# Two small weights in one tile: 64 runs of nine rows to every second partition, in place of 128 half runs to all of them

## The chip, the core and the metric

The kernel runs on one core of a Trainium2 chip. The metric is the time of one execution on the device in microseconds (us); smaller is better. The core has a matrix engine (TensorE, PE in the profile, with PEld for its weight loads), a vector engine (DVE), an activation engine (ACT), a general engine (POOL) and a queue engine (SP) that issues nearly all transfers. The transfers are carried by 16 DMA engines side by side. On-chip memory has 128 partitions.

## The reference

One decode step: a sum of an input, an attention block with a window of 2048 cached positions, and a mixing and feed-forward block, all on the normalized input. With batch B = 4, width D = 576, 32 query heads over 16 key heads of 128, F = 4608:

```
x  = A_x                                   # (4, 1, 576)
xn = layernorm(x)
# A: q = layernormed x @ wq; scores over the last 2048 of 8192 positions; softmax; p @ v; @ wo
# B: with h = gelu(layernorm(xn) @ w1)       w1: 576 x 576
#    hs = shift(h) @ w2                       w2: 576 x 576; four quarters of h, each shifted along the sequence
#    x1 = xn + hs
#    h2 = gelu(layernorm(x1) @ w3) @ w4       w3: 576 x 4608, w4: 4608 x 576
#    B  = x1 + h2
out = x + A + B
```

The sequence has length one, so every shift of h moves in zeros: the operand of w2 is zero for every input. The kernel still loads w2 and multiplies zeros (`hs_inT`) by it, and computes h.

## The kernel before

Everything is bf16 with fp32 accumulation. The work comes in an order written out by hand: each operation is put in a list of its engine with a sort key, the semaphores that it waits for and the one that it raises; each engine then runs its list in the order of the keys. The SP queue is such a list too, and an entry that waits holds up what is behind it.

The large transfers go to SP in this order: w1, w2, wq, w3, then 16 blocks of keys of 2 MB each (`k_cache`, into four slots of the tile `kring`, where wq lies in slots 2 and 3 at first), then 8 blocks of values of 4 MB each (into `vring` and `kring`), then w4 and five pieces of wo. Key blocks 2 and later wait for the product with wq (signal `q`), blocks 4 and later for the transposes of the block that had the slot, the first two value blocks for the product with w3 (`h2_1`), later ones for the products of the block before them in the slot; w4 and wo wait for value products near the end.

The weights w1, w2, wq and w3 are cut by the function `runs` into 128 runs: nine rows of the weight lie one behind the other in memory, and half of that stretch goes to each partition. For w1 and w2 a run is 4.5 rows, 5184 bytes. A partition then holds the first or the second half of nine rows, so the product's left operand must hold x for two rows at a time, with zeros in the places of the other parity: `pairs` picks the columns of x, `pe_xT` transposes five pieces of it (line 330), `xs_ops` writes two masked copies (line 336) with the parity mask `par`, and `x_at` gives the eight columns for each of the nine steps. `pe_hh` (line 397) computes x @ w1 in 9 matmuls of 288 columns, with the two column halves in rows 0 to 3 and 4 to 7 of the result (`HHps`, one PSUM bank). `pe_hs` (line 405) does the product with w2, two times 9 matmuls. The result of x @ w1 goes through gelu on ACT (line 415, `hh_sb`).

The order on PE at the start: a bank of zeros for q (line 360), the transposes for both layernorms (330), `pe_hh` (397), `pe_hs` for both halves (405) with DVE's sum into `x1_bf` (411) after each, the third layernorm, its transposes (330), the product with wq (369), q's transposes (380), zeros (360), the product with w3 (430), gelu and its transposes (443), zeros for the scores (347). Then come the loops: 16 key blocks (transposes in line 485, scores in line 492), a softmax, 8 value blocks (line 553), and at the end the products with w4 and wo (line 392).

w1 and w2 lie in the tile `ktb`, whose other half POOL sets to zero (line 239) at the start; the key loop uses all of `ktb` later on, and its first write there waits for the two products.

Of the kernel before, what the change touches and what calls it, by code (L numbers as in the profile page):

```python
# [6 lines left out]
BF16 = mybir.dt.bfloat16  # L7
ACTF = mybir.ActivationFunctionType
ALU = mybir.AluOpType
# [28 lines left out]
def bass_parallel_sum__sliding_block_cached__mixer_s_mlp__decode_kernel(  # L38
    nc, A_x, A_k_cache, A_v_cache, A_wq, A_wo, B_x, B_w1, B_w2, B_w3, B_w4, out
):  # L40
    B, Sq, D = A_x.shape
# [16 lines left out]
    HALF = D // 2  # L58
# [11 lines left out]
    with ExitStack() as ctx:  # L70
        def sb(name, shape, dt):
            return ctx.enter_context(nc.sbuf_tensor(name, shape, dt))
# [25 lines left out]
        def cut(n):  # L98
            nonlocal _o
            _o += n  # L100
            return ktb[:, _o - n:_o]
        w1_t = cut(9 * HALF)
        w2_t = cut(9 * HALF)
        assert _o <= NKT // 2 * 1024
        _o = 0
        PTx = vring[:, 4 * UE:4 * UE + 4 * 512].rearrange("p (q x) -> p q x", q=4)
# [9 lines left out]
        sd = sb("sd", [B, 3], FP32)  # L116
        rstd = sb("rstd", [B, 3], FP32)
        xn_bf = sb("xn_bf", [B, D], BF16)
        xp_bf = sb("xp_bf", [B, 3, 5 * 128], BF16)
        x1_bf = sb("x1_bf", [B, D], BF16)  # L120
        xs_t = sb("xs", [128, 3, 22 * B], BF16)
        par = sb("par", [128, 2], FP32)
        hs_inT = sb("hs_inT", [128, 9, 2, B], BF16)
        hh_sb = sb("hh_sb", [2 * B, HALF], BF16)
        h2_sb = sb("h2_sb", [128, 64 * 9], BF16)
        q_sb = vring[:, 5 * UE - 512:5 * UE]
        h2T_sb = sb("h2T_sb", [128, W4R, B], BF16)
# [2 lines left out]
        ident_bf = sb("ident_bf", [128, 128], BF16)  # L130
# [24 lines left out]
        ps = ctx.enter_context(nc.psum_tensor("ps", [128, 8, 512], FP32))[:]  # L155
# [3 lines left out]
        rinvps = ps[:, 5, 0:128]  # L159
        ORps = ps[:, 2, 0:128]  # L160
        ACC = [ps[32 * k:32 * k + B, 7, 0:HALF] for k in range(2)]
        Qps = ps[:, 4, :]
        QTps = ps[:, 0, 0:256].bitcast(BF16).rearrange("p (n j x) -> p n j x", n=4, j=4)
        HSps = ps[0:B, 5, 0:HALF]
        HHps = ps[0:2 * B, 3, 0:HALF]
        TS = ((0, 5), (5, 4))
        H2ps = [ps[:, 4 + k, 0:64 * n] for k, (_, n) in enumerate(TS)]
        H2Tps = ps[:, 1, 0:36 * B].rearrange("p (n j b) -> p n j b", n=9, j=4)
        XTps = [ps[:, k, 0:10].bitcast(BF16).rearrange("p (c b) -> p c b", b=B) for k in range(3)]

        S = {}
        for nm in ("pe", "dve", "act", "pool"):
# [15 lines left out]
        def add(engine, emit, waits=(), sig=None, key=0.0, inc=None):  # L188
            seqc[0] += 1
            prog[engine].append(Op(emit, waits, sig, key, seqc[0], inc))  # L190

        def add_dma(pairs, skey, waits=(), key=0.0, engine="sp"):
            if skey not in S:
                S[skey] = sem("s_" + "_".join(str(k) for k in (skey if isinstance(skey, tuple) else (skey,))))
            dma_count[skey] = dma_count.get(skey, 0) + 16 * len(pairs)

            def emit(e):
                for o_, i_ in pairs:
                    e.dma_start(o_, i_).then_inc(S[skey], 16)  # L199
            add(engine, emit, waits, None, key)  # L200
            return ("dma", skey, dma_count[skey])

        def runs(w_ap):
            return w_ap.rearrange("(m e) n -> m (e n)", e=9).rearrange("m (a x) -> (m a) x", a=2)

        for n in range(NB):
            ev_val[f"T{n}"] = ("T", n + 1)
# [18 lines left out]
        P = lambda *a, **k: add("pool", *a, **k)  # L226

        def pool_ident(t, tag, pattern, view, key):
            P(lambda e: e.memset(t[:], 1.0), sig=tag + "1", key=key)
            P(lambda e: e.affine_select(out=view, in_=view, compare_op=ALU.is_equal, fill=0.0, base=0,  # L230
                                        pattern=pattern, channel_multiplier=1), waits=[tag + "1"], sig=tag, key=key + 0.5)
        P(lambda e: e.memset(zeros_bf[:], 0.0), sig="zeros_bf", key=-100)
        pool_ident(ident_bf, "ident_bf", [[-1, 128]], ident_bf[:], -99)
        P(lambda e: e.memset(Qpad_t[:], 0.0), sig="qpad_zero", key=-96)
        P(lambda e: e.memset(hs_inT[:], 0.0), sig="hs_inT", key=-95.5)
        pool_ident(ident_f, "ident_f", [[-1, 128]], ident_f[:], -95)
# [13 lines left out]
        for gl in range(2):  # L250
            for x in range(2 * NVS):
                v = pick_bf[:, x, gl, 16 * gl:16 * gl + 16].rearrange("p (u r) -> p u r", u=NU)
                P(lambda e, v=v, x=x: e.affine_select(out=v, in_=v, compare_op=ALU.is_equal, fill=0.0, base=-(8 * (x // 2) + x % 2),
                                                      pattern=[[-NI, NU], [-2, 4]], channel_multiplier=1),
                  waits=["pick11"], sig=f"pick2{gl}{x}", key=-84 + 0.1 * (8 * gl + x))


        def mask_of(t, tag, view):
            add("dve", lambda e: e.tensor_reduce(out=t[:], in_=view, axis=AX.X, op=ALU.add), waits=["ident_f"], sig=tag, key=-8)
        add("dve", lambda e: e.tensor_reduce(out=par[:], in_=ident_f[:].rearrange("p (m a) -> p a m", a=2), axis=AX.X, op=ALU.add),  # L260
            waits=["ident_f"], sig="par", key=-29.5)
# [5 lines left out]

        ev_x = add_dma([(x_sb[:], x2)], "x", (), -100, engine="act")
        ev_wq = add_dma([(wq_t, runs(A_wq))], "wq", (), -48)
        ev_w1 = add_dma([(w1_t, runs(B_w1))], "w1", (), -50)  # L270
        ev_w2 = add_dma([(w2_t, runs(B_w2))], "w2", (), -49)
        ev_w3 = add_dma([(w3_t, runs(B_w3))], "w3", (), -47)
        ev_w4 = add_dma([(w4_t, B_w4.rearrange("(p r) n -> p r n", r=W4R))], "w4", [f"PV{2 * (NCV - NVS + 1) + 1}"], KS + NCV)

# [19 lines left out]
        ev_wo, WOR, a = [], [], 0  # L294
# [9 lines left out]
        def ln_ops(idx, src, dst, first_waits, tag, k0):  # L304
            add("dve", lambda e: (e.bn_stats(out=stats[:, idx, 0, :], in_=src[:, 0:HALF]),
                                  e.bn_stats(out=stats[:, idx, 1, :], in_=src[:, HALF:D]))[1],
                waits=first_waits, sig=f"{tag}_st", key=k0)
            add("dve", lambda e: e.bn_aggr(out=mv[:, idx, :], in_=stats[:, idx].rearrange("p a s -> p (a s)")),
                waits=[f"{tag}_st"], sig=f"{tag}_mv", key=k0 + 0.01)
            add("act", lambda e: e.activation(out=sd[:, idx:idx + 1], in_=mv[:, idx, 1:2], func=ACTF.Sqrt, bias=EPS, scale=1.0),  # L310
                waits=[f"{tag}_mv"], sig=f"{tag}_sd", key=k0 + 0.02)
            add("dve", lambda e: e.reciprocal(out=rstd[:, idx:idx + 1], in_=sd[:, idx:idx + 1]),
                waits=[f"{tag}_sd"], sig=f"{tag}_rstd", key=k0 + 0.03)
            add("dve", lambda e: e.tensor_scalar(out=dst[:] if idx == 0 else xp_v(idx), in0=src[:] if idx == 0 else pairs(src),  # L314
                                                 scalar1=mv[:, idx, 0:1], scalar2=rstd[:, idx:idx + 1],
                                                 op0=ALU.subtract, op1=ALU.mult), waits=[f"{tag}_rstd"], sig=f"{tag}_n" if idx == 0 else tag, key=k0 + 0.04)
            if idx == 0:
                add("dve", lambda e: e.tensor_copy(out=xp_v(0), in_=pairs(dst)), waits=[f"{tag}_n"], sig=tag, key=k0 + 0.05)

        xp_v = lambda idx: xp_bf[:, idx, :].rearrange("b (r m a) -> b r m a", r=5, a=2)  # L320

        def pairs(t):
            v = t[:]
            return bass.AP(tensor=v.tensor, offset=v.offset, ap=[list(v.ap[0]), [1, 5], [9, 64], [4, 2]])

        def pe_xT(idx):
            def f(e):
                ins = None
                for r in range(5):
                    ins = e.transpose(XTps[idx][:, r, :], xp_bf[:, idx, 128 * r:128 * (r + 1)], ident_bf[0:B, 0:B])  # L330
                return ins
            return f

        def xs_ops(idx, k0):
            for a in range(2):
                add("dve", lambda e, a=a: e.tensor_scalar(
                        out=xs_t[:, idx, 2 * B * (1 - a):2 * B * (11 - a)].rearrange("p (r v b) -> p r v b", v=4, b=B)[:, :, 0:4:3, :],
                        in0=XTps[idx].unsqueeze(2).to_broadcast([128, 5, 2, B]), scalar1=par[:, a:a + 1], scalar2=None, op0=ALU.mult),
                    waits=([f"xT{idx}"] + ([] if idx else ["par"])) if a == 0 else [], sig=f"xs{idx}{a}", key=k0 + 0.01 * a)

        def x_at(idx, s_):
            return xs_t[:, idx, 2 * B * (s_ + 1):2 * B * (s_ + 2)]

        def pe_zero(e):
            ins = None
# [38 lines left out]
        for k in range(2):  # L384
            for g in range(2):
                add("dve", lambda e, k=k, g=g: e.tensor_copy(
                        out=qp_out[:, :, 2 * k + g].rearrange("p b (j n) y -> p b j n y", j=2),
                        in_=QTps[:, :, 2 * g:2 * g + 2, B * k:B * (k + 1)].rearrange("p (n y) j b -> p b j n y", y=2)),
                    waits=["qTp"] + (["qpad_zero"] if k + g == 0 else []), sig=f"qT{2 * k + g}", key=-10 + 0.1 * k)
# [3 lines left out]

        def pe_hh(e):
            ins = None
            for s_ in range(9):
                ins = e.matmul(HHps, lhsT=x_at(1, s_), rhs=w1_t[:, HALF * s_:HALF * (s_ + 1)], start=(s_ == 0), stop=(s_ == 8))
            return ins
        add("pe", pe_hh, waits=[ev_w1, "xs10", "xs11"], sig="hT", key=-40)

        def pe_hs(h):
            def f(e):
                ins = None
                for s_ in range(9):
                    ins = e.matmul(HSps, lhsT=hs_inT[:, s_, h, :], rhs=w2_t[:, HALF * s_:HALF * (s_ + 1)], start=(s_ == 0), stop=(s_ == 8))
                return ins
            return f
        for h in range(2):
# [3 lines left out]
                waits=[f"hs{h}"], sig="x1" if h else "x1a", key=-27 + 0.1 * h)  # L412
# [3 lines left out]
            waits=["hT", "ln3_sd"], sig="gelu_h", key=-25.9)  # L416
# [30 lines left out]
        for k in range(2):  # L447
            add("pe", pe_h2(k), waits=[ev_w3] + (["xs20", "xs21", "gelu_h", "h2_zero"] if k == 0 else []), sig=f"h2_{k}", key=-18 + k)
            add("act", lambda e, k=k: e.activation(out=h2_v[k], in_=H2ps[k], func=ACTF.Gelu_apprx_tanh), waits=[f"h2_{k}"],
                sig=f"gelu2_{k}", key=-5 + 0.1 * k)  # L450
# [267 lines left out]
```

## Time and profile before

| | us |
|---|---|
| time, median of 3 runs | 213.94 (213.77 to 214.14) |
| the profiled execution's own time | 213.93 |
| its span, first to last instruction | 212.6 |

The profiled execution lies on the median; 1.3 us of its time are outside the span. In the profile's lines "PE L397" is a matrix product of line 397; SPq and ACTq are the queues that issue transfers; "x9" is a count. In a timeline the first two numbers are the start and the duration in us, and the brackets at the end tell how long the engine was idle before and what ended it. In the table of windows each engine has its busy time with its count of instructions, then come the granted clock, the mean busy share of the 16 DMA engines, and GB/s. A packet's bytes are counted where it is recorded, so that in short windows the share can be over 1.

### The profile page before, as it was taken

How to read it: one execution, taken by the hardware profiler on the slowest of the kernel's cores; microseconds unless marked ns; L12 is line 12 of the kernel's file. 1: busy time of each engine (PE TensorE's matmuls, PEld its weight loads, DVE VectorE, ACT ScalarE, POOL GpSimd, SP SyncE). 2: the span in 40 equal slices, each digit the busy share in tenths (PEclk: the TensorE clock that was granted, in tenths of full speed). 3: DMA queues.
4: the chain of work that ended last, by engine and by line, in shares of the span. 5: the costliest groups of instructions: out<-in, count | busy, mean ns of one | idle time of the engine just before them, and what ended most of it. 6: DMA issues, size and time to landing. Idle time of an engine off the chain costs nothing.

```text
span 212.6 us, 4856 instructions
## 1 busy us (share of the span) xinstructions
PE 172.5 (81%) x2212; PEld 133.7 (63%) x2216; DVE 111.9 (53%) x168; ACT 58.6 (28%) x69; POOL 15.6 (7%) x38
## 2 busy tenths in 40 slices
PE   1456147999999999999996089999989598997495
PEld 0222014888878888887774048988868487883262
DVE  5433200477776777777764869995575444003000
ACT  2004001366665566666656520000000000000000
POOL 8991000000000000000000000000000000000000
PEclk9997855899999999999999589999999889999799
DMA  6999999999999999999999999999999999999993
GB/s 242 453 444 445 429 396 416 432 425 427 429 416 438 432 422 429 435 422 424 432 444 438 444 407 459 413 425 453 407 444 438 419 425 410 451 476 393 407 408 131
DMA packets 5066, 88.65 MB, mean 417 GB/s; under 512 B 568, under 2 KB 704, under 8 KB 1216
## 3 DMA queue, kind: packets, MB, share of 16 engines
q1 hardware_dynamic: 5040, 88.49, 97.7%
q8 instruction: 8, 0.13, 0.3%
q14 instruction: 2, 0.02, 0.0%
q10 hardware_dynamic: 16, 0.01, 0.0%
HBM read 88.49 MB, written 0.00 MB: 416 GB/s over the span
## 4 chain that ended last, share of the span: by engine, by line
DMA 47%; PE 45%; DVE 4%; SPq 1%; ACT 1%; issue 1%
PE ps L485 23%; DMA vring<-in_A_wo_dram 15%; DMA vring<-in_B_w_dram 13%; DMA vring<-in_A_v_cache_dram 12%; PE ps L553 11%; DMA kring<-in_A_k_cache_dram 7%; PE ps L492 6%; PE ps L430 2%; SPq L199 1%; DVE vring L520 1%; DVE rmax L498 1%; DVE ktb L545 1%; PE ps L514 1%; PE ps L347 1%; ACT ktb L468 0%
## 5 line engine op out<-in xcount | busy, mean ns | idle before, releaser
L469 DVE COPY ktb<-ps 128x1024 bf16<-128x1024 bf16 x80 | 53.8, 689 | 23.5 <-PE ps L485 23.4
L485 PEld LDWEIGHTS ps<-perm_bf,kring 128*128 128x128 bf16 x1024 | 58.2, 98 | 8.3 <-issue 7.6
L485 PE MATMUL ps<-perm_bf,kring 128*128 128x128 bf16 x1024 | 61.7, 220 | 0.2
L468 ACT ACTIVATE ktb<-ps 128x1024 bf16<-128x1024 bf16 x48 | 48.0, 1023 | 32.5 <-PE ps L485 32.1
L545 DVE TENSOR_TENSOR ktb<-kring,mH_bf 128x4096 bf16<-128x4096 bf16 x16 | 36.2, 2286 | 14.6 <-PE ps L553 14.6
L553 PE MATMUL ps<-vring,ktb 128*128 128x256 bf16 x256 | 30.3, 282 | 4.3 <-DMA vring<-in_A_v_cache_dram 3.5
L553 PEld LDWEIGHTS ps<-vring,ktb 128*128 128x128 bf16 x256 | 25.7, 101 | 8.5 <-issue 3.6
L553 PE MATMUL ps<-kring,ktb 128*128 128x256 bf16 x256 | 28.6, 273 | 0.9 <-DMA kring<-in_A_v_cache_dram 0.9
L553 PEld LDWEIGHTS ps<-kring,ktb 128*128 128x128 bf16 x256 | 25.0, 98 | 4.5 <-issue 1.1
L608 ACT ACTIVATE out_sb<-ps 4x288 bf16<-4x288 f32 x1 | 0.4, 399 | 84.6 <-PE ps L392 84.6
L492 PE MATMUL ps<-ktb,Qs 128*32 128x512 bf16 x272 | 17.8, 382 | 1.2 <-ACT ktb L468 1.2
L430 PE MATMUL ps<-vring,xs 128*8 128x320 bf16 (+1 forms) x72 | 4.5, 429 | 7.6 <-DMA vring<-in_B_w_dram 7.6
L492 PEld LDWEIGHTS ps<-ktb,Qs 128*32 128x32 bf16 x272 | 5.7, 96 | 6.7 <-DVE ktb L469 1.4
L514 PE MATMUL ps<-vring,pick_bf 128*32 128x256 bf16 x64 | 3.9, 411 | 6.4 <-DVE rinv L532 6.4
L609 DVE CAST out_sb<-ps 4x288 bf16<-4x288 f32 x1 | 0.4, 449 | 15.7 <-PE ps L392 15.7
L392 PE MATMUL ps<-vring,h2T_sb 128*4 128x288 bf16 x72 | 6.2, 347 | 3.1 <-DMA vring<-in_B_w_dram 3.1
L571 DVE TENSOR_SCALAR tmp<-ps,maskd 128x128 f32<-128x128 f32 x2 | 0.7, 350 | 14.8 <-PE ps L553 14.8
L430 PEld LDWEIGHTS ps<-vring,xs 128*8 128x8 bf16 x72 | 2.1, 110 | 9.8 <-DMA vring<-in_B_w_dram 8.0
L330 PE MATMUL ps<-ident_bf,xp_bf 4*128 4x4 bf16 x15 | 0.8, 163 | 8.1 <-DVE xp_bf L314 5.0
L392 PEld LDWEIGHTS ps<-vring,h2T_sb 128*4 128x4 bf16 x72 | 3.7, 101 | 5.8 <-DMA vring<-in_B_w_dram 3.6
L514 PEld LDWEIGHTS ps<-vring,pick_bf 128*32 128x32 bf16 x64 | 2.0, 118 | 8.2 <-DVE rinv L532 6.9
L239 POOL MEMSET ktb<- 128x8192 bf16 x1 | 6.9, 6924 | 0.0
(93 smaller groups left out, 78.6 us busy)
## 6 DMA issues: line engine op xcount, KB each, us to landing
kring<-in_A_k_cache_dram SPq DMA_DIRECT2D x16, 2048.0 KB, 13.8
vring<-in_A_v_cache_dram SPq DMA_DIRECT2D x4, 4096.0 KB, 24.6
kring<-in_A_v_cache_dram SPq DMA_DIRECT2D x3, 4096.0 KB, 34.0
vring<-in_B_w_dram SPq DMA_DIRECT2D x2, 5184.0 KB, 25.1
kring<-in_A_wq_dram SPq DMA_DIRECT2D x1, 4608.0 KB, 15.7
kring<-in_A_v_cache_dram SPq DMA_DIRECT2D x2, 2048.0 KB, 27.4
vring<-in_A_wo_dram SPq DMA_DIRECT2D x1, 1872.0 KB, 26.9
vring<-in_A_wo_dram SPq DMA_DIRECT2D x1, 1440.0 KB, 29.8
```

Of the source, the lines that this page charges most:

```text
L199: e.dma_start(o_, i_).then_inc(S[skey], 16)
L239: P(lambda e: e.memset(ktb[:, NKT // 2 * 1024:NKT * 1024], 0.0), key=-92, inc=(("E", LB - 2), 1))
L347: ins = e.matmul(ps[:, w, :], lhsT=zeros_bf[:, 0:128], rhs=zeros_bf[:, :], start=True, stop=True)
L392: return e.matmul(ACC[h], lhsT=lhsT, rhs=rhs, start=start, stop=stop, tile_position=(0, 32 * h), skip_group_check=True)
L430: ins = e.matmul(H2ps[k][32 * j:32 * j + 2 * B].rearrange("b (p t) -> b p t", t=n), lhsT=x_at(2, s_), rhs=w[:, :, 9 * j + t0:9 * j + t0 + ...
L468: return "act", lambda e: e.activation(out=ktbuf[:, n % NKT], in_=tb[n % 4], func=ACTF.Copy)
L469: return "dve", lambda e: e.tensor_copy(out=ktbuf[:, n % NKT], in_=tb[n % 4])
L485: ins = e.transpose(tb[j % 4][:, t, :], kslot_t(k)[:, 8 * kb + t, :], perm_bf[:])
L492: ins = e.matmul(Sps[32 * u:32 * u + 32, q, :].rearrange("p (t i) -> p t i", t=16), lhsT=Qs[:, k, 32 * u:32 * u + 32], rhs=ktgrp[:, (4 * k ...
L514: ins = e.matmul(ps[32 * j:32 * j + 32, 4 + qt, 256 * ih:256 * (ih + 1)].rearrange("p (t a e) -> p t a e", a=NPAIR, e=2), lhsT=pick_bf[:, ...
L545: return lambda e: e.tensor_tensor(out=PTpad[:, n % 4], in0=PTv[:, qt, NH * h:NH * (h + 1), bp, :].unsqueeze(2).to_broadcast([128, NH, NX, ...
L553: ins = e.matmul(ps[:, 0, 0:256], lhsT=PTpad[:, 2 * (k % 2) + h, 2 * g:2 * g + 2].rearrange("p t h e -> p (t h e)"), rhs=vslot(k)[:, Dh * ...
```

## The change

w1 and w2 are no longer cut in half runs. Each goes in 64 runs of nine whole rows, 10368 bytes, w1 to the even partitions and w2 to the odd partitions of one tile, `w12_t`. The tile has the same number of bytes per partition as the two tiles before.

A product over all 128 partitions therefore meets both weights. For w1 the left operand holds x on the even partitions and zeros on the odd ones: POOL sets a new tile `xw_bf` to zero first, the second layernorm writes to every second place of it (`nines` picks the columns), nine transposes in place of five bring it to `xw_t`, and one DVE copy takes the place of the two masked ones. `pe_hh` needs 18 matmuls, nine for each half of the columns, into two PSUM banks, and waits for w2 as well as for w1. For w2 the operand is zero everywhere, as before. The gelu covers 4 partitions with 576 columns in place of 8 with 288. The result of q moves to another PSUM bank.

```diff
-        w1_t = cut(9 * HALF)
-        w2_t = cut(9 * HALF)
+        w12_t = cut(9 * D)
...
-        xp_bf = sb("xp_bf", [B, 3, 5 * 128], BF16)
+        xp_bf = sb("xp_bf", [B, 2, 5 * 128], BF16)
+        xw_bf = sb("xw_bf", [B, 9, 64, 2], BF16)
+        xw_t = sb("xw", [128, 9, B], BF16)
...
-        hs_inT = sb("hs_inT", [128, 9, 2, B], BF16)
-        hh_sb = sb("hh_sb", [2 * B, HALF], BF16)
+        hs_inT = sb("hs_inT", [128, 9, B], BF16)
+        hh_sb = sb("hh_sb", [B, 2, HALF], BF16)
...
-        Qps = ps[:, 4, :]
+        Qps = ps[:, 6, :]
...
-        HHps = ps[0:2 * B, 3, 0:HALF]
+        HHps = ps[0:B, 3:5, 0:HALF]
...
+        def rows9(w_ap):
+            return w_ap.rearrange("(m e) n -> m (e n)", e=9)
+
         def runs(w_ap):
-            return w_ap.rearrange("(m e) n -> m (e n)", e=9).rearrange("m (a x) -> (m a) x", a=2)
+            return rows9(w_ap).rearrange("m (a x) -> (m a) x", a=2)
...
+        P(lambda e: e.memset(xw_bf[:], 0.0), sig="xw_zero", key=-97)
         P(lambda e: e.memset(Qpad_t[:], 0.0), sig="qpad_zero", key=-96)
...
-        ev_w1 = add_dma([(w1_t, runs(B_w1))], "w1", (), -50)
-        ev_w2 = add_dma([(w2_t, runs(B_w2))], "w2", (), -49)
+        ev_w1 = add_dma([(w12_t[0:128:2], rows9(B_w1))], "w1", (), -50)
+        ev_w2 = add_dma([(w12_t[1:128:2], rows9(B_w2))], "w2", (), -49)
...
+        def nines(t):
+            v = t[:]
+            return bass.AP(tensor=v.tensor, offset=v.offset, ap=[list(v.ap[0]), [1, 9], [9, 64]])
+
         def pe_xT(idx):
+            src = xw_bf[:].rearrange("b e m a -> b (e m a)") if idx == 1 else xp_bf[:, idx // 2, :]
...
-                for r in range(5):
-                    ins = e.transpose(XTps[idx][:, r, :], xp_bf[:, idx, 128 * r:128 * (r + 1)], ident_bf[0:B, 0:B])
+                for r in range(9 if idx == 1 else 5):
+                    ins = e.transpose(XTps[idx][:, r, :], src[:, 128 * r:128 * (r + 1)], ident_bf[0:B, 0:B])
...
         def xs_ops(idx, k0):
+            if idx == 1:
+                add("dve", lambda e: e.tensor_copy(out=xw_t[:], in_=XTps[1]), waits=["xT1"], sig="xw", key=k0)
+                return
...
-            for s_ in range(9):
-                ins = e.matmul(HHps, lhsT=x_at(1, s_), rhs=w1_t[:, HALF * s_:HALF * (s_ + 1)], start=(s_ == 0), stop=(s_ == 8))
+            for h in range(2):
+                for s_ in range(9):
+                    ins = e.matmul(HHps[:, h, :], lhsT=xw_t[:, s_, :], rhs=w12_t[:, D * s_ + HALF * h:D * s_ + HALF * (h + 1)],
+                                   start=(s_ == 0), stop=(s_ == 8))
             return ins
-        add("pe", pe_hh, waits=[ev_w1, "xs10", "xs11"], sig="hT", key=-40)
+        add("pe", pe_hh, waits=[ev_w1, ev_w2, "xw"], sig="hT", key=-40)
...
-                    ins = e.matmul(HSps, lhsT=hs_inT[:, s_, h, :], rhs=w2_t[:, HALF * s_:HALF * (s_ + 1)], start=(s_ == 0), stop=(s_ == 8))
+                    ins = e.matmul(HSps, lhsT=hs_inT[:, s_, :], rhs=w12_t[:, D * s_ + HALF * h:D * s_ + HALF * (h + 1)], start=(s_ == 0), stop=(s_ == 8))
```

More of the change, by code (lines that the diff above doesn't have):

```diff
@@ L118, in bass_parallel_sum__sliding_block_cached__mixer_s_mlp__decode_kernel @@
         xn_bf = sb("xn_bf", [B, D], BF16)
-        xp_bf = sb("xp_bf", [B, 3, 5 * 128], BF16)
+        xp_bf = sb("xp_bf", [B, 2, 5 * 128], BF16)
+        xw_bf = sb("xw_bf", [B, 9, 64, 2], BF16)
+        xw_t = sb("xw", [128, 9, B], BF16)
         x1_bf = sb("x1_bf", [B, D], BF16)
-        xs_t = sb("xs", [128, 3, 22 * B], BF16)
+        xs_t = sb("xs", [128, 2, 22 * B], BF16)
         par = sb("par", [128, 2], FP32)
-        hs_inT = sb("hs_inT", [128, 9, 2, B], BF16)
-        hh_sb = sb("hh_sb", [2 * B, HALF], BF16)
+        hs_inT = sb("hs_inT", [128, 9, B], BF16)
+        hh_sb = sb("hh_sb", [B, 2, HALF], BF16)
         h2_sb = sb("h2_sb", [128, 64 * 9], BF16)
@@ L168, in bass_parallel_sum__sliding_block_cached__mixer_s_mlp__decode_kernel @@
         H2Tps = ps[:, 1, 0:36 * B].rearrange("p (n j b) -> p n j b", n=9, j=4)
-        XTps = [ps[:, k, 0:10].bitcast(BF16).rearrange("p (c b) -> p c b", b=B) for k in range(3)]
+        XTps = [ps[:, k, 0:2 * n].bitcast(BF16).rearrange("p (c b) -> p c b", b=B) for k, n in enumerate((5, 9, 5))]
         S = {}
@@ L313, in ln_ops @@
                 waits=[f"{tag}_sd"], sig=f"{tag}_rstd", key=k0 + 0.03)
-            add("dve", lambda e: e.tensor_scalar(out=dst[:] if idx == 0 else xp_v(idx), in0=src[:] if idx == 0 else pairs(src),
+            add("dve", lambda e: e.tensor_scalar(out=dst[:] if idx == 0 else xw_bf[:, :, :, 0] if idx == 1 else xp_v(idx),
+                                                 in0=src[:] if idx == 0 else nines(src) if idx == 1 else pairs(src),
                                                  scalar1=mv[:, idx, 0:1], scalar2=rstd[:, idx:idx + 1],
-                                                 op0=ALU.subtract, op1=ALU.mult), waits=[f"{tag}_rstd"], sig=f"{tag}_n" if idx == 0 else tag, key=k0 + 0.04)
+                                                 op0=ALU.subtract, op1=ALU.mult), waits=[f"{tag}_rstd"] + (["xw_zero"] if idx == 1 else []), sig=f"{tag}_n" if idx == 0 else tag, key=k0 + 0.04)
             if idx == 0:
                 add("dve", lambda e: e.tensor_copy(out=xp_v(0), in_=pairs(dst)), waits=[f"{tag}_n"], sig=tag, key=k0 + 0.05)
-        xp_v = lambda idx: xp_bf[:, idx, :].rearrange("b (r m a) -> b r m a", r=5, a=2)
+        xp_v = lambda idx: xp_bf[:, idx // 2, :].rearrange("b (r m a) -> b r m a", r=5, a=2)
         def pairs(t):
@@ L334, in xs_ops @@
         def xs_ops(idx, k0):
+            if idx == 1:
+                add("dve", lambda e: e.tensor_copy(out=xw_t[:], in_=XTps[1]), waits=["xT1"], sig="xw", key=k0)
+                return
             for a in range(2):
                 add("dve", lambda e, a=a: e.tensor_scalar(
-                        out=xs_t[:, idx, 2 * B * (1 - a):2 * B * (11 - a)].rearrange("p (r v b) -> p r v b", v=4, b=B)[:, :, 0:4:3, :],
+                        out=xs_t[:, idx // 2, 2 * B * (1 - a):2 * B * (11 - a)].rearrange("p (r v b) -> p r v b", v=4, b=B)[:, :, 0:4:3, :],
                         in0=XTps[idx].unsqueeze(2).to_broadcast([128, 5, 2, B]), scalar1=par[:, a:a + 1], scalar2=None, op0=ALU.mult),
@@ L341, in x_at @@
         def x_at(idx, s_):
-            return xs_t[:, idx, 2 * B * (s_ + 1):2 * B * (s_ + 2)]
+            return xs_t[:, idx // 2, 2 * B * (s_ + 1):2 * B * (s_ + 2)]
         def pe_zero(e):
```

## The prediction, made before the result was known

> **What bounds the kernel now.** I read first the page's second and third parts: what the 16 DMA engines did over the span, and what each queue moved.
>
> ```profile
> span 212.6 us, 4856 instructions
> ...
> DMA  6999999999999999999999999999999999999993
> ...
> DMA packets 5066, 88.65 MB, mean 417 GB/s; under 512 B 568, under 2 KB 704, under 8 KB 1216
> ...
> q1 hardware_dynamic: 5040, 88.49, 97.7%
> ```
>
> The DMA row holds a 9 in every slice but the first and the last: the 16 engines never run dry. The queue of SP, q1, moves 88.49 MB and fills 97.7% of the engines' time. So the kernel takes as long as its bytes take, plus some 2 us before the first of them and 3 after the last. To see whether that holds in each stage I take the windows, where the last three columns are the granted clock, the share of the DMA engines and GB/s:
>
> ```profile
> core 0: us, PE busy (x) PEld busy (x) DVE busy (x) ACT busy (x) POOL busy (x), PEclk, DMA share, GB/s
> 1.50:2.50 1.00, 0.48 (x1) 0.00 (x0) 0.26 (x1) 1.00 (x1) 0.97 (x2) 1.00 0.64 150
> 2.50:5.00 2.50, 0.00 (x0) 0.00 (x0) 2.13 (x7) 0.39 (x2) 2.35 (x7) 1.00 1.03 406
> 6.20:20.00 13.80, 8.29 (x73) 4.04 (x73) 5.88 (x17) 1.88 (x3) 10.32 (x23) 0.94 1.01 434
> 20.00:94.00 74.00, 64.45 (x1062) 51.38 (x1056) 41.90 (x80) 35.88 (x38) 0.00 (x0) 0.90 1.00 425
> 178.00:208.00 30.00, 25.81 (x254) 18.79 (x255) 2.53 (x6) 0.00 (x0) 0.00 (x0) 0.94 1.00 425
> ```
>
> From 2.5 us on every stage has a share of 1.00 or more, at 406 to 434 GB/s, while the matrix engine's load changes from nothing to nearly everything. Third, the chain of waits in order of time (start, length, what):
>
> ```profile
> 2.17 27.46 DMA vring<-in_B_w_dram
> 29.63 0.04 issue
> 29.68 4.52 PE ps L430 x56
> ...
> 92.14 2.35 PE ps L485 x40
> 94.49 0.02 issue
> 94.51 14.58 DMA kring<-in_A_k_cache_dram
> ...
> 142.08 25.49 DMA vring<-in_A_v_cache_dram
> ...
> 178.35 31.68 DMA vring<-in_A_wo_dram
> ```
>
> It begins with w3, which stands in the queue behind w1, w2 and wq and lands at 29.63. In between there are stretches of PE work, but each DMA link is far longer than the transfer itself: the 2048 KB block issued at 94.51 needs about 5 us at 425 GB/s and lands after 14.58, because others stand before it. A link like that is a full queue. So whatever the change adds to or takes from the time in which w1 and w2 go through the engines moves w3, the keys, the values and the end by the same amount; what it does elsewhere counts only if it makes an issue so late that the queue empties.
>
> **The transfers of w1 and w2.** What they take now:
>
> ```profile
> L199 SPq DMA_DIRECT2D ktb<-in_B_w_dram x2: 374/395/416, 0.8 to 1.2; - x2
> ...
> DMA to landing us min/median/max: 3.6/4.3/5.0
> ```
>
> w1 is issued at 0.80 and lands 3.6 us later at 4.4, w2 is issued at 1.24 and lands 5.0 later, at 6.2. Together they are 2 x 648 KB = 1.327 MB. The bytes stay the same; 256 packets of 5184 bytes become 128 of 10368, and each transfer now goes to 64 partitions in place of 128.
>
> Half as many packets: the window with nothing but w1 and w2 in it (2.5 to 5.0) runs at 406 GB/s, the ones with large rows at 425 to 434. If the longer runs closed the whole gap to 434, 1.327 MB would take 3.06 us in place of 3.27: a gain of 0.2. I take 0.1, the middle between that and nothing.
>
> Half as many partitions: this is the term that decides, and no row shows it. Every large transfer of this kernel writes all 128 partitions. The fastest long window, 434 GB/s, is 3.4 GB/s for one partition. To keep its time the change needs 6.8 GB/s for each partition that it writes, twice what any row shows. Bounds: at one end nothing is lost, because the engines are the limit and not the place that they write to; at the other end a partition takes no more than it is seen to take. At that end, w1 and w2 go at half of 406, 203 GB/s. In the window from 1.5 to 2.5 only 0.15 MB arrive, at 150 GB/s, less than that half, so those bytes lose nothing. The other 1.177 MB take 5.80 us in place of 2.90: a loss of 2.9 us (3.3 if nothing hides at the start). I take a value near this end, because it is what the rows nearest to it bear out: 16 engines together have been seen to write to 128 partitions only. I don't take all of it. [...] Loss: 2.9 - 0.4 = 2.5 us, with 0 and 3.3 as ends.
>
> [...]
>
> **The work on the engines.** All of it lies between the landing of w2 and the landing of w3. The rows that carry the path and its cover:
>
> ```profile
> 7.39 0.29 PE L330 MATMUL ps<-ident_bf,xp_bf 4*128 4x4 bf16 x5 [1.98 <-DVE xp_bf L314]
> 8.46 2.32 PE L397 MATMUL ps<-ktb,xs 128*8 128x288 bf16 x9 [0.78 <-DVE xs L336]
> 17.32 0.40 ACT L415 ACTIVATE hh_sb<-ps 8x288 bf16<-8x288 f32 x1
> 17.41 3.06 PE L369 MATMUL ps<-kring,xs 128*8 128x512 bf16 x36
> 21.57 0.54 PE L360 MATMUL ps<-zeros_bf 128*128 128x320 bf16 x2
> 29.68 4.49 PE L430 MATMUL ps<-vring,xs 128*8 128x320 bf16 x72 [7.56 <-DMA vring<-in_B_w_dram]
> 36.26 1.49 PE L347 MATMUL ps<-zeros_bf 128*128 128x512 bf16 x3 [0.81 <-DVE h2T_sb L452]
> ```
>
> - Wait added: `pe_hh` also waits for w2. Now w2 lands at 6.2 and the product starts at 8.46, held by x. In the slow case w2 lands at about 8.7 to 9.5, so up to 1.0 us later; queued behind it on PE are the product with w2, the third layernorm's transposes and the product with wq.
> - Matmuls: 18 of 288 columns in place of 9. The 9 take 2.32 us at the start; at that price the others add 2.3.
> - Transposes: 9 in place of 5, at 0.29 for 5: +0.24. The gelu has 576 columns in place of 288, at most twice 0.40: +0.4, beside the transposes and the product with wq.
>
> Sum on PE's path: 1.0 + 2.3 + 0.2 + 0.4 = 3.9 us at most. PE sits idle for 7.56 us before the product with w3, waiting for w3's landing and for nothing else. So it costs nothing, with 3.6 us to spare, and more in the slow case, where w3 lands later as well. Were the cover gone, each us would be paid in full.
>
> What is issued later: the third key block waits in SP's queue for the end of the product with wq, and all later issues stand behind it.
>
> ```profile
> SPq L199 <- PE ps L369: 16.5, 1, 16.5
> ...
> 1.78 1.83 POOL L234 MEMSET Qpad<- 128x2080 bf16 x1
> 3.91 0.40 POOL L230 TENSOR_SCALAR_AFFINE_SELECT ident_f<-ident_f 128x128 f32<-128x128 f32 x1
> 5.54 6.92 POOL L239 MEMSET ktb<- 128x8192 bf16 x1
> 13.84 2.80 POOL L253 TENSOR_SCALAR_AFFINE_SELECT pick_bf<-pick_bf 128x16 bf16<-128x16 bf16 x16
> ...
> 6.41 0.93 DVE L314 TENSOR_SCALAR xp_bf<-xn_bf,mv,rstd 4x640 bf16<-4x640 bf16 x1
> 7.64 0.68 DVE L336 TENSOR_SCALAR xs<-ps,par 128x40 bf16<-128x40 bf16 x4
> ```
>
> That wait ends at 17.41 + 3.06 = 20.5, by the sum above at 24.4 at the latest. In the queue then stand what is left of w3, until 29.63, and two key blocks, 2 x 5 us: the engines have work until about 39. 15 us of cover; nothing lost.
>
> POOL's new fill of `xw_bf` has 1152 elements per partition; at Qpad's 1.83 us for 2080 that is 1.0 us. It stands ahead of Qpad, so all of POOL's later work comes 1.0 later. The second layernorm's write (6.41) needs the fill by then and has it at about 2.8. The parity mask, on DVE just before the copies at 7.64, needs `ident_f`, ready at 4.31, then 5.3. The zeros in `ktb` end at 13.5 in place of 12.46 and are needed by the key loop, which starts after 36.26 + 1.49. The last selection ends at 17.6 and is needed after the keys. Nothing lost. On DVE one copy of 36 columns replaces two masked ones of 40: at most 0.3 us gained, into the same cover. The moved PSUM bank has no price, and the space per partition is the same.
>
> **The sum**, against the profiled execution's own 213.93, which lies on the median of 213.94: +2.5 for the partitions, -0.1 for the packets, 0 for the rest: 216.3 us.
>
> **The rivals.** *The engines are the limit, not the partitions.* For it: the rate hardly depends on what is transferred, 425 in the key stage and 425 at the end, and 64 rows can still be dealt to 16 engines, four each. Against: no row has a partition taking 6.8 GB/s. Then only the packets count: 213.93 - 0.1 = 213.8, no change. [...] That the transfer is cut in other pieces than the diff says, and so isn't changed at all, ends here too. Chance 0.29.
>
> *Faster: long runs pay more than I give them.* w2 lands 1.8 us after w1 (6.2 against 4.4), where its bytes need 1.53 us at 434 GB/s. If that 0.27 us goes for both transfers, the end comes 0.5 us earlier: 213.4. Against: each landing is that of the last of 16 engines, so the gap holds their spread too, which longer runs need not narrow. Chance 0.11.
>
> *Slower by PE.* If the path of 3.9 us grew beyond 7.56, the product with w3 and the key loop, in which PE works without a gap until 94.5, would come later. But the queue is full there, so only what then empties it counts: 1 us beyond the cover gives at most 214.9. It needs a wait that I don't see. Chance 0.04.
>
> **How the numbers follow.** My forecast, half the partitions at about half the rate, has 0.56; its own range goes from half of the loss, 1.4, to the whole of 3.3: 215.3 to 217.2. With the first rival it holds 0.85; the range that takes in both goes from 213.5 to 217.2. Below it lies the faster case. About 0.2%, 0.43 us, is what a measurement of this kernel can tell from no change; the three runs before differ by 0.37. Faster: 0.11. Same: 0.29. Slower: 0.56 + 0.04 = 0.60.
>
> **What would show it.** Right: w2 lands near 8.7 in place of 6.2, the windows from 2.5 to 8 show about 200 to 250 GB/s, w3 lands near 32, and the DMA links of the chain keep their lengths while each starts 2.5 us later. PE's idle time before the product with w3 stays between 5 and 8 us. The prediction is wrong if w3 lands within 0.3 us of 29.6, if the added time appears in the key or value stage instead, or if PE doesn't wait for w3.

## The result, and the profile after

The changed kernel takes 215.00 us in the median of 8 runs (214.47 to 215.71) against 213.97 for the kernel before: a ratio of 1.0053, 95% interval 1.0038 to 1.0067. It is slower by 1.0 us, clear of noise, where 2.4 was forecast. Its runs also spread more: 1.2 us from the fastest to the slowest, where before's have 0.4. The profiled execution took 215.69, near the slow end of them, with a span of 214.4; a second profile of the same kernel, further down, took 215.03.

The page's parts on the span and the transfers:

```profile
span 214.4 us, 4882 instructions
...
DMA  6999989999999999999999999999999999999991
...
DMA packets 4938, 88.65 MB, mean 413 GB/s; under 512 B 568, under 2 KB 704, under 8 KB 960
...
q1 hardware_dynamic: 4912, 88.49, 97.0%
```

The same 88.49 MB in 128 packets fewer, and an 8 now stands in the sixth slice of the row. The windows, with the columns of before:

```profile
1.50:2.50 1.00, 0.49 (x1) 0.00 (x0) 0.04 (x1) 1.00 (x1) 0.96 (x2) 1.00 0.54 119
2.50:5.00 2.50, 0.00 (x0) 0.00 (x0) 2.12 (x6) 0.39 (x2) 2.44 (x4) 1.00 0.91 365
2.50:8.00 5.50, 0.27 (x5) 0.21 (x5) 4.79 (x11) 0.59 (x3) 5.29 (x10) 1.00 1.09 415
6.20:20.00 13.80, 7.64 (x50) 4.28 (x50) 5.64 (x16) 1.69 (x4) 11.34 (x24) 1.00 0.94 400
20.00:94.00 74.00, 65.30 (x1081) 50.72 (x1080) 42.25 (x82) 36.20 (x39) 0.00 (x0) 0.93 1.00 427
178.00:208.00 30.00, 25.41 (x241) 18.86 (x245) 1.93 (x6) 0.00 (x0) 0.00 (x0) 0.94 1.00 428
```

From 20 us on the rate is that of before (427 for 425, 428 for 425): the loss is made ahead of that. But w1 and w2 don't go at half rate: 365 GB/s in place of 406 in their window, and 119 in place of 150 in the one before. The window from 6.2 to 20, which is mostly wq's, has 400 in place of 434: one engine lands w2 1.9 us after the middle one of the 16 and one lands wq 1.4 us after the middle one (in the kernel before 0.4 for both), and wq's first packets take longer too (up to 2380 ns, in the kernel before up to 1974). The transfers themselves, with the key issues of before in the first row, and the chain:

```profile
L199 SPq DMA_DIRECT2D kring<-in_A_k_cache_dram x16: 534/535/616, 2.7 to 94.5; - x16
...
L200 SPq DMA_DIRECT2D kring<-in_A_k_cache_dram x16: 534/535/1640, 3.1 to 95.2; - x16
...
L200 SPq DMA_DIRECT2D ktb<-in_B_w_dram x2: 553/562/571, 0.8 to 1.4; - x2
...
DMA to landing us min/median/max: 4.0/5.3/6.7
```

```profile
2.66 28.80 DMA vring<-in_B_w_dram
31.45 0.04 issue
31.50 4.25 PE ps L447 x52
...
75.87 14.45 DMA kring<-in_A_k_cache_dram
...
142.93 25.70 DMA vring<-in_A_v_cache_dram
...
178.22 34.02 DMA vring<-in_A_wo_dram
```

An issue of 64 runs occupies SP for 0.55 to 0.57 us where one of 128 took 0.37 to 0.42. w1 lands at 0.8 + 4.0 = 4.8 in place of 4.4, w2 at 1.4 + 6.7 = 8.1 in place of 6.2, w3 at 31.45 in place of 29.63. One of the key issues took 1640 ns where none took more than 616 before: SP was held up. The later links of the keys and the values keep about their lengths (14.45 for 14.58, 25.70 for 25.49). The last one doesn't, 34.02 for 31.68: it is another piece of wo, and by the semaphore records one engine lands that piece at 212.25 where the other 15 have it by 211.44. So part of what this execution takes over the median comes from its very end.

The work on the engines came out as the prediction priced it:

```profile
1.78 1.05 POOL L238 MEMSET xw_bf<- 4x1152 bf16 x1
...
8.37 0.40 PE L342 MATMUL ps<-ident_bf,xw_bf 4*128 4x4 bf16 x9 [2.35 <-DVE xw_bf L319]
9.22 4.48 PE L413 MATMUL ps<-ktb,xw 128*4 128x288 bf16 x18 [0.46 <-DVE xw L348]
...
20.00 0.64 ACT L432 ACTIVATE hh_sb<-ps 4x576 bf16<-4x576 f32 x1
...
PE ps L447 <- DMA vring<-in_B_w_dram: 6.8, 1, 6.8
```

The fill takes 1.05 us (1.0 was estimated), the 18 matmuls 4.48 (2.3 + 2.3), the gelu 0.64. PE still waits 6.8 us for w3.

The views show only the last of 16 engines to land a transfer. Read out of the trace's packet and semaphore records, for the two small weights (a transfer "lands" on each engine by itself; a packet's record doesn't name its engine):

```
kernel               packet  median ns  slowest   second transfer lands, first to last engine
before               5184 B     199        831      5.70 to 6.22
changed             10368 B     389       1304      6.05 to 8.14
e4, changed again   10368 B     396       1435      5.93 to 7.47
e1 transfers alone  10368 B     392       1219      6.00 to 7.45
e3 two halves       10368 B     780        824      8.79 to 9.15
e7 behind wq        10368 B     389        389     16.68 to 17.29
```

In the changed kernel most packets take 389 ns, hardly less than two of before's 199. But while the second transfer runs one packet takes 1304 ns (1435 in e4), and one engine lands that transfer 1.9 us (1.4 in e4) after the middle one of the 16. In e1 it is two engines. By the semaphore records each of the large transfers behind them has 16 landings of its own as well, so an engine that is late can stay so to the end: in e4's profile, an execution of 215.03 us, the 16 engines land the last piece of wo 0.4 us later than before's in the mean, and the last of them 1.2 us later.

### The profile page after: what moved, and what is told of

Read it like the earlier page. It is cut to its first block, busy times and chain, and to the rows that moved or that the text cites. A ratio compares the mean times of both kernels' runs of the same rounds, so it can differ in the third digit from the quotient of the medians.

```text
span 214.4 us, 4882 instructions
## 1 busy us (share of the span) xinstructions
PE 172.0 (80%) x2225; PEld 133.2 (62%) x2229; DVE 112.6 (53%) x167; ACT 59.3 (28%) x69; POOL 16.7 (8%) x39
## 3 DMA queue, kind: packets, MB, share of 16 engines
q1 hardware_dynamic: 4912, 88.49, 97.0%
HBM read 88.49 MB, written 0.00 MB: 413 GB/s over the span
## 4 chain that ended last, share of the span: by engine, by line
DMA 55%; PE 36%; DVE 4%; SPq 2%; ACT 1%; issue 1%
PE ps L502 17%; DMA vring<-in_A_wo_dram 16%; DMA kring<-in_A_k_cache_dram 14%; DMA vring<-in_B_w_dram 13%; DMA vring<-in_A_v_cache_dram 12%; PE ps L570 10%; PE ps L509 5%; PE ps L447 2%; SPq L200 2%; DVE vring L537 1%; DVE rmax L515 1%; DVE ktb L562 1%; PE ps L531 1%; ACT ktb L485 0%; PE ps L362 0%
## 5 line engine op out<-in xcount | busy, mean ns | idle before, releaser
L502 PEld LDWEIGHTS ps<-perm_bf,kring 128*128 128x128 bf16 x1024 | 57.4, 98 | 8.7 <-issue 7.1
L570 PE MATMUL ps<-vring,ktb 128*128 128x256 bf16 x256 | 28.6, 273 | 4.5 <-DMA vring<-in_A_v_cache_dram 3.7
L570 PEld LDWEIGHTS ps<-vring,ktb 128*128 128x128 bf16 x256 | 24.8, 98 | 7.9 <-issue 3.6
```

Source lines behind the costliest of these rows:

```text
L502: ins = e.transpose(tb[j % 4][:, t, :], kslot_t(k)[:, 8 * kb + t, :], perm_bf[:])
L570: ins = e.matmul(ps[:, 0, 0:256], lhsT=PTpad[:, 2 * (k % 2) + h, 2 * g:2 * g + 2].rearrange("p t h e -> p (t h e)"), rhs=vslot(k)[:, Dh * ...
```

## The experiments

Each was timed against the kernel before on the same chip; its medians there were 213.71 to 213.97. The theory at first: the loss lies in the transfers, in the start and not in the partitions' rate. The rivals: the partitions' rate (the prediction's term), and the added work on the engines.

**Transfers alone, work alone (e1, e2).** e1 is the kernel before with this:

```diff
-        ev_w1 = add_dma([(w1_t, runs(B_w1))], "w1", (), -50)
-        ev_w2 = add_dma([(w2_t, runs(B_w2))], "w2", (), -49)
+        ev_w1 = add_dma([(w12_t[0:128:2], rows9(B_w1))], "w1", (), -50)
+        ev_w2 = add_dma([(w12_t[1:128:2], rows9(B_w2))], "w2", (), -49)
```

(`w1_t` and `w2_t` are now the two halves of that tile's columns, and `pe_hh` also waits for w2.)

> The kernel before with the changed transfers alone: w1 and w2 go as 64 runs of nine rows to alternate partitions; the products stay the old 9 steps of 288 columns over that tile, so x @ w1 is not what the reference has. If the whole loss lies in the transfers (my theory), this is as slow as the changed kernel: 1.0 us over before (214.8 to 215.5), w2 lands near 8 us and w3 near 31 us. If it lies in the longer work on PE and POOL (rival), it stays at before's 214.0, with w3 at 29.6.

Measured: 214.97 us, ratio 1.0047 (1.0030 to 1.0065), with w2 landing at 7.45 and w3 at 30.64. e2 is the changed kernel with the opposite edit (`w12_t[:, 0:9 * HALF]` and `runs(B_w1)`, and so for w2):

> The changed kernel with the transfers of before: 128 half runs of w1 and w2 to all partitions; the 18 matmuls, nine transposes and the fill of the changed kernel stay, over a layout that they do not fit, so x @ w1 is not what the reference has. If the transfers are the whole loss: 214.0, as before, with w3 at 29.6. If the added work costs, up to 215.0.

Measured: 213.98 us, ratio 1.0002 (0.9993 to 1.0010). The whole loss is in the transfers; the added work costs nothing. One sign was missed, the landing of w3:

```profile
2.17 28.84 DMA vring<-in_B_w_dram
31.01 0.04 issue
```

It comes at 31.01, almost as late as in the changed kernel, and the end is that of the kernel before. By the semaphore records 15 of the 16 engines have w3 by 29.56, and one is 1.4 us later. A fetch of 16 KB of instructions, 0.94 us long, is on record at 23.0; the kernel before has its first such fetch at 33.6, and there one engine lands the first key block 1.2 us after the others (35.70). That such a fetch holds up one engine fits, but isn't shown. So a late landing of w3 is no proof of a loss: it is the landing of one engine of 16, and at the end another may be the last.

**The changed kernel again (e4)**, without an edit:

> The changed kernel unchanged, for a second profile: its eight times lie between 214.47 and 215.71. If one late engine in w2 (landing 8.1 in the first profile) belongs to the layout, w2 lands near 8 again; if that was chance, it lands near 6.6, 0.35 after before's, and the profiled time is near 214.5.

Measured: 215.15 us (214.28 to 216.24), ratio 1.0061 (1.0042 to 1.0080); w2 landed at 7.5, and a key issue took 1111 ns. The late engine is no chance of one profile.

**Halves in place of alternate partitions (e3)**, to see whether it matters where the 64 partitions lie:

```diff
-        ev_w1 = add_dma([(w12_t[0:128:2], rows9(B_w1))], "w1", (), -50)
-        ev_w2 = add_dma([(w12_t[1:128:2], rows9(B_w2))], "w2", (), -49)
+        ev_w1 = add_dma([(w12_t[0:64], rows9(B_w1))], "w1", (), -50)
+        ev_w2 = add_dma([(w12_t[64:128], rows9(B_w2))], "w2", (), -49)
...
-        xw_bf = sb("xw_bf", [B, 9, 64, 2], BF16)
+        xw_bf = sb("xw_bf", [B, 9, 2, 64], BF16)
```

> The changed kernel with w1 on partitions 0 to 63 and w2 on 64 to 127 in place of even and odd ones; all products as in the changed kernel. [...] If the loss is only a late start and one late engine, whatever the partitions are: 215.0, as the changed kernel.

Measured: 216.72 us, ratio 1.0125 (1.0111 to 1.0140): 2.8 us slower than before. The window of w1 and w2, that of the kernel before first, and e3's landings:

```profile
2.50:8.00 5.50, 0.56 (x10) 0.42 (x10) 4.67 (x15) 0.59 (x3) 5.29 (x9) 1.00 1.08 429
...
2.50:8.00 5.50, 0.27 (x5) 0.21 (x5) 4.79 (x11) 0.59 (x3) 5.29 (x10) 1.00 1.06 245
...
DMA to landing us min/median/max: 5.2/6.5/7.7
```

This is the half rate of the prediction, at nearly the size that it gave (2.5): 245 GB/s in place of 429, each packet 780 ns in place of 389, w2 at 9.1. (16 packets of 10368 bytes in 780 ns are 213 GB/s; the end of the window has the first of wq in it.) But it belongs to neighbours. Alternate partitions don't have it.

**Half runs on the alternate partitions (e5)**, to see whether the long packets matter: the tile gets 64 more columns, and each partition's row is cut in two.

```diff
-        w12_t = cut(9 * D)
+        w12_t = cut(9 * D + 64)
...
-        ev_w1 = add_dma([(w12_t[0:128:2], rows9(B_w1))], "w1", (), -50)
+        ev_w1 = add_dma([(w12_t[0:128:2].rearrange("m (a x) -> m a x", a=2)[:, :, 0:9 * HALF],
+                          rows9(B_w1).rearrange("m (a x) -> m a x", a=2))], "w1", (), -50)
```

(and so for w2, with the products' columns moved along)

> The changed kernel with the same 64 alternate partitions, but each partition's nine rows come in two runs of 5184 bytes with a gap of 64 bytes between them, so there are 128 packets per transfer again. If the long packets make one engine late, it is gone and the time is near before's plus the later start, 214.3. If the 64 partitions do (fewer rows per engine, other places), 215.0, with w2's landing at 7.4 or later.

Measured: 215.01 us, ratio 1.0056 (1.0044 to 1.0069), w2 landing at 7.4. The loss doesn't come from the length of the packets.

**The other one first (e6)**: the keys of w1 and w2 in the queue exchanged.

> The changed kernel with w2 issued ahead of w1. If the late engine belongs to what is second in the queue, 215.0 again, with the second transfer's landing at 7.4 to 8.1 and the first's at 4.8. If it belongs to w2's rows or the odd partitions, the first transfer lands late, near 6, and the second near 7.

Measured: 214.80 us, ratio 1.0053 (1.0036 to 1.0069). The second transfer, now w1, lands at 1.4 + 6.5 = 7.9. The first lands at 5.1, somewhat late. What is second is hit, whichever weight it is and on even or odd partitions.

**Another place in the queue (e7, e8, e10, e12).** e7: the changed kernel with `"wq", (), -48` turned into `-51`, so that wq goes first. e8: the same in the kernel before.

> The changed kernel with wq issued first, then w1, w2, w3. If the loss is a late start of the first transfer (an issue of 0.55 us in place of 0.37) it vanishes, since wq's issue is not longer: 214.0 or e8's time. If the late engine comes with these transfers wherever they stand, 0.5 to 1.0 over e8. PE gets to the product with w3 later, by about 3 us after w3's landing; the queue stays full, so I expect no cost of that.

> The kernel before with wq issued first, the control for e7: 214.0 if the order of the first four transfers does not matter, as the full queue says.

Measured: e7 213.97 us, ratio 1.0003 (0.9994 to 1.0011); e8 214.04, ratio 1.0008 (0.9999 to 1.0017). The loss is gone. A window inside w1 and w2, that of e8 first, and e7's landings, then PE:

```profile
13.90:15.40 1.50, 0.00 (x0) 0.00 (x0) 0.00 (x0) 0.00 (x0) 1.50 (x9) 1.00 1.03 429
...
13.90:15.40 1.50, 0.00 (x0) 0.00 (x0) 0.00 (x0) 0.00 (x0) 1.37 (x7) 1.00 1.03 435
...
DMA to landing us min/median/max: 14.5/15.0/15.5
...
32.93 3.55 PE L447 MATMUL ps<-vring,xs 128*8 128x320 bf16 x72
```

435 GB/s to 64 alternate partitions is 6.8 GB/s for each, the rate that no row of before had; the same window of e8, with 128 partitions, has 429. (Towards its end some engines are at w2 already, on the other 64 partitions. The middle engine lands w2 1.56 us after w1, which is four packets of 389 ns, and the first packet of w1 starts at 13.25: up to 14.8 no engine should be at w2, and from 13.80 to 14.80 the rate is 435 too.) The last row shows something more: the product with w3 starts at 32.93, 3.3 us later than in the kernel before, and w3 has been there since 29.6. PE is 3.3 us late at the key loop, and that costs nothing.

e12 puts the halves of e3 behind wq:

> The version on partitions 0 to 63 and 64 to 127, with wq issued first. If neighbours share ways into the memory wherever the transfer stands in the queue, the loss is that of the first such run, about 2.8: 216.8. If that loss too came from the start, 214.0.

Measured: 217.45 us, ratio 1.0166 (1.0151 to 1.0181). That is 3.5 us over before, more than the 2.8 that I expected; the packets take 780 ns here too. The neighbours' loss is there in either place in the queue.

e10 leaves w1 first and moves only w2 behind wq (key -47.5 in place of -49):

> The changed kernel with the order w1, wq, w2, w3. If each of the two transfers at the start costs by itself (late start by w1, one late engine in w2), only the late start is left: 214.2 to 214.3. If one transfer of 64 runs at the start is enough for the whole loss, 215.0.

Measured: 213.98 us, ratio 1.0004 (0.9995 to 1.0012). I had expected the late start to stay, and it doesn't:

```profile
L200 SPq DMA_DIRECT2D kring<-in_A_k_cache_dram x16: 534/535/620, 3.3 to 95.8; - x16
L200 SPq DMA_DIRECT2D ktb<-in_B_w_dram x2: 482/520/558, 0.8 to 2.0; - x2
...
DMA to landing us min/median/max: 3.8/9.5/15.3
```

w1's issue is as long as in the changed kernel (558 ns) and it lands at 4.6, later than before's 4.4, but no key issue is held up, and w2, from 2.0, lands at 17.3. By the packet records no packet of wq takes over 1591 ns there, where before's first ones take up to 1974 and the changed kernel's up to 2380, with 1364 as the usual time: what the start loses is made good at wq.

**A late start by itself (e9)**: the kernel before, w1's entry with the wait `["zeros_bf"]`, POOL's first fill.

> The kernel before, its first issue (w1) held until POOL's first fill is done at 1.3 us, so that everything on SP starts about 0.5 us later. If the full queue hands a late start on, the end is later by as much: 214.4 to 214.5, and the 0.2 to 0.3 us by which the changed kernel's first transfers come later are paid in full. If later stages make up for it, 214.0.

Measured: 214.40 us, ratio 1.0025 (1.0015 to 1.0034), so 0.5 us (0.3 to 0.7) for a start that is 0.55 later (first issue at 1.35 in place of 0.80). The queue hands it on here.

**Two queues (e11)**: w2's entry with `engine="act"`, behind x.

> The changed kernel with w2 issued from ACT's queue, right behind x, in place of SP's behind w1. If engines run out of work between w1 and w2 because SP's queue hands it out too slowly, two queues fill the gap: 214.3 or less, w2 lands by 6.5, and SP's second key issue is no longer held up. If the slow engine is slow by itself, 215.0.

Measured: 214.53 us (214.01 to 215.85), ratio 1.0039 (1.0024 to 1.0054). The interval reaches into that of the changed kernel; in its profile, a run of 214.01, no key issue is over 647 ns. w2 landed at 10.6, where 6.5 was expected: wq was issued at the same time. It doesn't decide.

**What else is in the queue at that time (e13, e14, e15).** e13: w3 waits for w1's landing (`[ev_w1]`). e14: wq does. e15: w2's issue waits for x's (`[ev_x]`).

> The changed kernel, with the issue of w3 and all behind it on SP held until w1 has landed (4.7 us); wq is queued and keeps the engines busy until 17. If the issues on top slow an engine down: 214.0 to 214.2. If the pair does it by itself: 215.0, and w2 lands at 7.4 or later.

> The same with wq held too, so that w1 and w2 are alone in the queue until 4.7. wq's first bytes come about 1 us after its issue, near 5.8, when w2 ends at 5.9: no gap to speak of. If the issues on top slow an engine down: 214.0 to 214.4, with w2's landing near 6.3. If the pair does it by itself: 215.0 or more.

> The changed kernel with w2's issue held until x has landed (2.3 us), 0.9 us later than in the changed kernel; w1 keeps the engines busy until 4.3. If the two issues come too close together, the loss shrinks: 214.2 to 214.5. If the engines wait for a late supply of w2, it grows: over 215.2. If neither, 215.0.

Measured: e13 215.80 us, ratio 1.0081 (1.0051 to 1.0111), w2 at 1.4 + 6.8 = 8.2; e14 215.20, ratio 1.0071 (1.0056 to 1.0086), w2 at 1.4 + 6.7 = 8.1; e15 214.62, ratio 1.0037 (1.0024 to 1.0050), w2 at 2.2 + 4.5 = 6.7. In e14 nothing but w1 and w2 is queued on SP until 4.5, and an engine is late all the same: the pair does it by itself. Two issues further apart may lessen it; the interval of e15 touches that of the changed kernel, so that is not shown. In e15's profile the last engine lands w2 only 0.4 us after the middle one, and e15 is still 0.5 to 1.1 us slower than before.

## Why the prediction was right or wrong

Right: the way the profile was read. The kernel is bound by its queue of transfers; the loss arises with w1 and w2 and in wq's stretch behind them and is carried to the end, with the rate of the stages from 20 us on unchanged (427 and 428 GB/s for 425); the added matmuls, transposes, fill and gelu cost nothing (e2: 1.0002), at prices that the trace confirms. Slower came out too, but not by the mechanism that was priced, so that is luck.

Wrong: the step "Half as many partitions: this is the term that decides". It put 2.5 us on the argument that a partition takes no more than it has been seen to take. For alternate partitions that term is nil: e7 writes to 64 of them at 435 GB/s, and its total is before's. The rate per partition in the trace (3.4 GB/s) was no limit, only what 16 engines gave when they served 128. The forecast 216.3 is what the kernel would have done, nearly, with w1 and w2 on neighbouring partitions (e3, 216.72). The rows could not tell the two layouts apart; taking the end that the nearest row "bears out" was a choice without a row behind it, and the first rival, "the engines are the limit, not the partitions", had that step right. No run shows the 0.4 us that the sum takes off the 2.9 of the half rate: e3, at 245 GB/s from 2.5 to 8 us, is 2.8 us slower than before.

Three of the signs that the prediction named came out near all the same: w2's landing (8.1 for 8.7), w3's (31.45 for 32) and PE's wait (6.8, between 5 and 8). Those landings are the last of 16 engines. Against it spoke the rate from 2.5 to 8, 415 GB/s in place of 200 to 250, and the link of the values in the chain, which starts 0.85 us later (142.93 for 142.08) in place of 2.5.

Missing from the sum: the start. The prediction left the issues as they were. They take 0.55 to 0.57 us in place of 0.37 to 0.42, w1's landing moves by 0.3 to 0.4, and e9 shows that such a delay is paid in full when nothing makes it good. And it had no term for an engine that falls behind: one or two engines of 16 are late in the second of two 64-run transfers at the head of the queue, and in the changed kernel's profiles the last engine sets the end. Of 1.0 us the first is about 0.3 by e9's slope, the rest about 0.7, worked out as a difference and not measured by itself; e4's profile (0.4 in the mean of the engines, 1.2 in the last) agrees with that. In e15, where w2 lands 0.6 us later in the mean and no engine is so late, the same working gives 0.5, and 0.9 (0.5 to 1.1) was measured. So the size of the parts is not shown. Both go when wq stands between or ahead (e10, e7). Packets gained the forecast's 0.1 at the most: 389 ns for two times 199, or 9 ns in each of 8 packets an engine.

The sentence that each us beyond the cover would be paid in full was wrong as well. In e7 and e10 PE starts the product with w3 3.3 and 3.7 us after w3 has landed, and the end doesn't move; the queue is full at that point, which the prediction itself says in its rival of a slower PE.

Open: why an engine is late in the second transfer. It goes with a held-up key issue in every profile of the plain pair (1111 to 1891 ns), but e14, where the keys come later, is slow with 728. Whether the engine waits for its orders or for its data, the records don't tell. No version beat the kernel before; e7 and e10 equal it.

## What to carry to other kernels

When a kernel is bound by its queue of transfers, look at each engine's share and at the queue's first microseconds: a late engine or a late start can be carried to the end (e4, the last engine 1.2 us late there; e9, 0.5 us for a start 0.55 later), while work on the compute engines can slip by microseconds unnoticed (e7, 3.3 us). The landing of one transfer is that of its last engine and may mislead (e2, w3 at 31.01 and the end that of before). Here the transfers to 64 partitions were not slow by their number: where the partitions lay decided (389 ns a packet on alternate ones in e7, 780 on neighbours in e3), and a small experiment with neighbours against alternate ones showed it. Here a transfer of 4608 KB ahead of two short ones, or between them, took the whole loss away (e7 213.97 us, e10 213.98); that is worth a try at the head of another queue. And where no row of the profile holds the term that decides, let the forecast stay between its ends.

## What the runs showed of the hardware that was not expected

- The transfers to 64 neighbouring partitions went at half rate: 780 ns a packet for 389, at the head of the queue and behind wq (e3, e12). On alternate partitions a packet took 389 ns and a window had 435 GB/s (e7).
- An issue of 64 runs took longer than one of 128: 0.55 us for 0.37 at the head of the queue, 0.54 for 0.42 behind wq (e7, e8), and an unchanged issue took longer behind two of them (wq 578 ns for 424).
- Two such transfers at the head of the queue made one or two engines late, the last of them by 1.2 to 1.9 us behind the middle one (the changed kernel, e4, e1, e5, e6), with packets of 5184 bytes (e5) as with 10368. With one of them at the head the time was that of the kernel before (e10, 213.98 us), and with both behind wq the 16 engines landed the second within 0.6 us (e7).
